# One instruction for a half block's normalization, ScalarE for the first output copies, and block 4's attention kept to the second group

## The chip, the cores and the metric

The program runs on one core of a Trainium2 chip. The metric is the time of one execution on the device, in microseconds; the median of several runs is quoted, and a profiled execution supplies the traces.

## What is computed

Attention over pooled keys and values, then a layer x -> (h cos h) with h = x w_in, then w_out, then a mixture of eight experts whose gate is balanced by eight rounds of row and column scaling. The change touches the first two stages:

```python
k_p = k.reshape(B, H, Sp, pool, D).mean(axis=3)
v_p = v.reshape(B, H, Sp, pool, D).mean(axis=3)
scores = scale * np.matmul(q, k_p.transpose(0, 1, 3, 2))
scores = scores - np.max(scores, axis=-1, keepdims=True)
attn = np.exp(scores)
attn = attn / (np.sum(attn, axis=-1, keepdims=True) + 1e-09)
out = np.matmul(attn, v_p)
...
h = x @ w_in
g = h * np.cos(h)
return g @ w_out
```

with 4 batches, 8 heads, 576 tokens, heads of 64, a pool of 8 (so 72 keys), and hidden widths of 2048 here and 1024 in each expert.

## The kernel before

The 2304 tokens are cut into six blocks of 384. Blocks 0 to 3 are the first group, 4 and 5 the second. Within a group the loop runs over four units of 512 hidden columns and, in each, over the group's blocks; one (unit, block) pair is a task, so the first group is tasks 0 to 15 and the second 16 to 23. A task is `hidden1` four times (f0 to f3: twelve matmuls each, in three passes of split fp32, then cosine work on ScalarE and VectorE, then the low part gl on GpSimd) and `output1` (four output chunks of twelve matmuls, added to `acc`). A task's `output1` is issued in the next task, behind its f0. f1 and f3 write the PSUM banks `ps_s`, which the attention's scores use too; f0 and f2 write `ps_h`.

Beside the tasks two queues are drained. `attn_queue` holds, for the blocks 1 to 5 and two half blocks g each (four heads), `attn_weights` (scores, maximum, exponential, sum, `normalize`) and `attn_values` (transposes and the product with the values); neighbours are swapped so that the weights of the next half block come ahead of the values of this one. `ATT` says how many entries a task takes at its start: 5, 4 and 4 in tasks 0 to 2, none in tasks 3 to 7, and one each from task 8 on, until the queue is empty. `conv_queue` turns the 64-bit weights of later units into fp32: two pieces per task in tasks 0 to 11, by ScalarE, five VectorE instructions, one GpSimd instruction (cw, L126) and a write to DRAM (`wa1f`, `wb1f`), from where `load_unit` fetches them for the first block of a unit.

The keys and values of a batch are pooled when a block first needs them: `load_k` issues four loads of 288 KB (kr), sums each on GpSimd in three instructions (L200 twice, L202) and copies the result by ScalarE into the block-diagonal tile kbd (L207) that the scores multiply; `load_v` does the like for values (vr, vs). Batch 3 is first needed by block 4. These loads and the raw weight tiles share one pool, `rawp`, of three buffers, and all are issued on SP's queue. `split` (L94 on ScalarE, L95 on GpSimd) makes the high and low part of a raw weight tile.

Each engine runs its instructions in the order that the tile scheduler wrote down when the program was built: it simulates the program and moves instructions, so an edit in one place moves others.

```python
engine = nc.vector if n > 4 else nc.gpsimd
for i in range(0, n, 4):
    r = slice(i, i + 4)
    engine.tensor_tensor(out=at[:, r], in0=at[:, r], in1=rs[:, r].to_broadcast([P, 4, SP]), op=ALU.mult)
```

Of the kernel before, what the change touches and what calls it, by code (L numbers as in the profile page):

```python
# [14 lines left out]
AF = mybir.ActivationFunctionType  # L15
ALU = mybir.AluOpType
# [4 lines left out]
SP = S // POOL  # L21
HP = H // 2
P = 128
# [7 lines left out]
NBLK = T // NB  # L31
# [27 lines left out]
def fused_kernel(ctx: ExitStack, tc: tile.TileContext, qT, kT, vT, v0, wa1, wb1, wa2, wb2, wg, out):  # L59
    nc = tc.nc  # L60
# [69 lines left out]
    def mm3(ps, pairs, part=None):  # L130

        n = len(pairs)
        for i in range(n) if part is None else part:
            (lh, ll), (rh, rl) = pairs[i]
            nc.tensor.matmul(out=ps, lhsT=lh, rhs=rh, start=(i == 0), stop=False)  # L135
            nc.tensor.matmul(out=ps, lhsT=lh, rhs=rl, start=False, stop=False)  # L136
            nc.tensor.matmul(out=ps, lhsT=ll, rhs=rh, start=False, stop=(i == n - 1))  # L137

    def mm3_first(ps, pairs):

        mm3(ps[0], pairs[0], range(FC - 1))
        mm3(ps[1], pairs[1], range(FC - 1))
        mm3(ps[0], pairs[0], range(FC - 1, FC))
        mm3(ps[1], pairs[1], range(FC - 1, FC))

    def x_tiles(j):
        hi = xp.tile([P, KC, NB], F32R, tag=f"xh{j}", name=f"xh{j}")
        lo = xp.tile([P, KC, NB], F32R, tag=f"xl{j}", name=f"xl{j}")
        return hi, lo
# [136 lines left out]
    def normalize(at, sm):  # L286

        nc.vector.tensor_scalar(
            out=sm, in0=sm, scalar1=EPS, scalar2=float(POOL), op0=ALU.add, op1=ALU.mult
        )  # L290
        n = sm.shape[1]
        rs = sp.tile([P, TPB * 4, 1], F32, tag="rs", name="rs")[:, :n]
        nc.vector.reciprocal(out=rs, in_=sm)
        engine = nc.vector if n > 4 else nc.gpsimd
        for i in range(0, n, 4):
            r = slice(i, i + 4)
            engine.tensor_tensor(out=at[:, r], in0=at[:, r], in1=rs[:, r].to_broadcast([P, 4, SP]), op=ALU.mult)  # L297

    ats = {}
    xts = {}  # L300
# [6 lines left out]
    def attn_first(qcs, g):  # L307

        at = at_tile(0, g)
        for i in range(TPB):  # L310
            ps = scores(i, g, qcs[i][:, 2 * g:2 * g + 2], (ps_s, "ps") if i % 2 == 0 else (ps_a, "pa"))
            mx = sp.tile([P, 4, 1], F32, tag="mx", name="mx")
            nc.vector.tensor_reduce(out=mx.rearrange("p h o -> p (h o)"), in_=ps, op=ALU.max, axis=AX.X,
                                    negate=True)
            nc.vector.tensor_scalar(out=mx, in0=mx, scalar1=SCALE, scalar2=None, op0=ALU.mult)
            sm = sp.tile([P, 4, 1], F32, tag="sm0", name="sm0")
            for h in range(4):
                nc.scalar.activation(out=at[:, i, h, :], in_=ps[:, h, :], func=AF.Exp, scale=SCALE,
                                     bias=mx[:, h, :], accum_out=sm[:, h, :])
            normalize(at[:, i], sm)  # L320

    def attn_weights(j, g):

        at = at_tile(j, g)
        for i in range(TPB):
            c = j * TPB + i
            for _, _, b in batch_runs(c * P, P):
                if b not in kpool:
                    load_k(b)
            qc = qp.tile([P, 2, P], F32, tag="qc", name="qc")  # L330
            nc.sync.dma_start(out=qc, in_=qT[:, c, 2 * g:2 * g + 2])
            ps = scores(c, g, qc)
            mx = sp.tile([P, 4, 1], F32, tag="mx", name="mx")
            nc.vector.tensor_reduce(out=mx.rearrange("p h o -> p (h o)"), in_=ps, op=ALU.max, axis=AX.X)
            nc.vector.tensor_tensor(out=at[:, i], in0=ps, in1=mx.to_broadcast([P, 4, SP]), op=ALU.subtract)
        nc.scalar.activation(out=at, in_=at, func=AF.Exp, scale=SCALE)
        sm = sp.tile([P, TPB * 4, 1], F32, tag="sm", name="sm")
        nc.vector.tensor_reduce(out=sm.rearrange("p h o -> p (h o)"), in_=at, op=ALU.add, axis=AX.X)
        normalize(at.rearrange("p c h s -> p (c h) s"), sm)
# [53 lines left out]
    def output1(j, u, gs, w_b, acc):  # L393

        last = u == U1 - 1
        if last:
            nhi, nlo = x_tiles(j)
        pss = {}

        def product(c):  # L400
            return [((w_b[f][0][:, c * P:(c + 1) * P], w_b[f][1][:, c * P:(c + 1) * P]), gs[f]) for f in range(FC)]

        for c in range(KC):
            if c == 0:
                for cc in range(2):
                    pss[cc] = ps_o.tile([P, 512], F32, tag="po", name="po")[:, :NB]
                mm3_first([pss[0], pss[1]], [product(0), product(1)])
            elif c > 1:
                pss[c] = ps_o.tile([P, 512], F32, tag="po", name="po")[:, :NB]
                mm3(pss[c], product(c))  # L410
            ps = pss[c]
            a = acc[:, c, :]
            if u == 0:
                nc.vector.tensor_copy(out=a, in_=ps)
            else:
                nc.vector.tensor_tensor(out=a, in0=ps, in1=a, op=ALU.add)
            if last:
                nc.scalar.activation(out=nhi[:, c, :], in_=a, func=AF.Copy)
                nc.vector.tensor_tensor(
                    out=nlo[:, c, :], in0=a, in1=nhi[:, c, :].bitcast(F32), op=ALU.subtract  # L420
                )
        if last:
            x1[j] = (nhi, nlo)
            if j > 1:
                nc.sync.dma_start(out=x1f[j], in_=acc)

    GRP = [[0, 1, 2, 3], [4, 5]]
# [9 lines left out]
    def convert_piece(u, i, raw=None):  # L437
        if raw is None:
            raw = load_piece(u, i)
        return convert(raw, (wa1f, wb1f)[i // FC], u, i % FC)  # L440

    attn_queue = [lambda f=f, j=j, g=g: f(j, g) for j in range(1, NBLK) for g in range(2)
                  for f in (attn_weights, attn_values)]

    for i in range(1, len(attn_queue) - 1, 2):
        attn_queue[i:i + 2] = attn_queue[i + 1], attn_queue[i]
    conv_queue = [lambda u=u, i=i: convert_piece(u, i) for u in range(1, U1) for i in range(2 * FC)]

    def run(queue, n):
        for _ in range(min(n, len(queue))):  # L450
            queue.pop(0)()
# [292 lines left out]
    pending = None  # L744
    task = 0

    ATT = [5, 4, 4, 0, 0, 0, 0, 0]
    accs = {}
    side = []
    for gi, grp in enumerate(GRP):  # L750
# [3 lines left out]
        for u in range(U1):  # L754
            for j in grp:
# [6 lines left out]
                if u == 0:  # L762
                    accs[j] = accp.tile([P, KC, NB], F32, tag="acc", name="acc")
                run(attn_queue, ATT[task] if task < len(ATT) else 1)
                gs = []
                for f in range(FC):
# [12 lines left out]
                    if f == 0 and j == GRP[1][1] and u == U1 - 1:  # L779
                        side.append(lambda: logits(GRP[1][0]))  # L780
                pending = lambda j=j, u=u, gs=gs, w=w_b, a=accs[j]: output1(j, u, gs, w, a)
                if gi == 1 and u == 0 and j == grp[0]:
                    x_op, x_load, x_todo = x_pieces(0)
# [11 lines left out]
    for _ in range(2):  # L795

        ps = ps_s.tile([P, 512], F32, tag="ps", name="pset")
# [94 lines left out]
```

## Time and profile before

| | us |
|---|---|
| median of 3 runs | 2053.98 (2053.37 to 2056.27) |
| the profiled execution | 2056.55 |
| its span, first to last instruction | 2054.7 |
| TensorE busy in the span | 2008.2 |
| VectorE / ScalarE / GpSimd busy | 1254.5 / 899.3 / 818.1 |

PE is TensorE, PEld its weight loads, DVE VectorE, ACT ScalarE, POOL GpSimd, SPq the DMA queue of SP. Names such as gl<-r,gh are the program's tiles, output first. A figure in brackets behind a row is how long the engine stood idle before it, and what released it. Matmuls are pipelined, so their starts tell their pace.

### The profile page before, as it was taken

Reading aid. Unit: us, or ns where it says so; the run is one execution under the profiler, and the core shown is the slowest. Engines: PE = TensorE matmul, PEld = TensorE weight load, DVE = VectorE, ACT = ScalarE, POOL = GpSimd, SP = SyncE. Lnnn points to the kernel's source line nnn. Section 1 sums busy time; section 2 is a strip of 40 time slices with the busy share of each in tenths; the row PEclk is TensorE's granted clock in tenths of the full one; section 3 lists DMA queues with packets and bytes.
Section 4 is the critical chain, followed back from the end, with each engine's and each line's share of the span. In section 5 each row is a group of like instructions: output and inputs, shape, how many; then the busy total and the mean of one; then the engine's idle time right before and its main releaser. Section 6 shows DMA issues by size and latency. Waiting matters only on the chain.

```text
span 2054.7 us, 27450 instructions
## 1 busy us (share of the span) xinstructions
PE 2008.2 (98%) x10339; PEld 1817.8 (88%) x10339; DVE 1254.5 (61%) x2003; ACT 899.3 (44%) x1781; POOL 818.1 (40%) x646
## 2 busy tenths in 40 slices
PE   6799999999999999999999999999999999999999
PEld 5689899999888889989888888888898888898887
DVE  8987785655685555555666555555565655555553
ACT  6675566656533334333444343343343343333431
POOL 7755653433333234243443342342353432433420
PEclk8899999999999999999999999999999999999999
DMA  7433331211311212212232122121132221221210
GB/s 257 140 126 124 110 121 47 83 52 62 123 63 62 68 56 82 62 62 74 70 123 72 52 83 72 52 82 62 62 107 92 69 72 54 80 72 52 83 42 31
DMA packets 53636, 167.46 MB, mean 81 GB/s; under 512 B 6112, under 2 KB 9952, under 8 KB 53504
## 3 DMA queue, kind: packets, MB, share of 16 engines
q1 hardware_dynamic: 53504, 165.72, 24.9%
q8 instruction: 81, 1.33, 0.3%
q14 instruction: 51, 0.42, 0.1%
HBM read 149.44 MB, written 16.25 MB: 81 GB/s over the span
## 4 chain that ended last, share of the span: by engine, by line
PE 88%; DVE 5%; DMA 1%; ACT 1%; issue 1%; POOL 1%; SPq 0%; DVEq 0%; ACTq 0%; POOLq 0%
PE po L135 15%; PE po L136 15%; PE po L137 15%; PE py L683 14%; PE pv L683 10%; PE px L683 10%; PE ph L136 2%; PE ph L135 2%; PE ph L137 2%; DVE m L121 1%; DVE at L297 1%; DVE cw L125 0%; DMA wb1f<-cw 0%; DVE m L119 0%; DVE r L387 0%
## 5 line engine op out<-in xcount | busy, mean ns | idle before, releaser
L95 POOL TENSOR_TENSOR wlo<-raw,whi 128x512 fp32r<-128x512 f32 x248 | 345.2, 1410 | 680.9 <-ACT gh L671 489.6
L135 PE MATMUL po<-whi,gh 128*128 128x512 f32 x1152 | 455.1, 395 | 0.6 <-DVE acc L733 0.6
L136 PE MATMUL po<-wlo,gh 128*128 128x512 f32 x1152 | 454.4, 394 | 0.0
L137 PE MATMUL po<-whi,gl 128*128 128x512 f32 x1152 | 454.0, 394 | 0.0
L94 ACT ACTIVATE whi<-raw 128x512 fp32r<-128x512 f32 x488 | 290.3, 625 | 220.6 <-PE py L683 184.8
L739 DVE SCALAR_TENSOR_TENSOR acc<-po,pr,acc 128x512 f32<-128x512 f32 x252 | 188.7, 749 | 292.4 <-PE po L137 288.2
L683 PE MATMUL py<-xc,whi 128*128 128x384 f32 x1152 | 293.7, 335 | 0.0
L95 DVE TENSOR_TENSOR wlo<-raw,whi 128x512 fp32r<-128x512 f32 x240 | 216.7, 903 | 125.6 <-ACT whi L94 60.5
L137 PEld LDWEIGHTS po<-whi,gl 128*128 128x128 f32 x1152 | 216.2, 188 | 50.1
L135 PEld LDWEIGHTS po<-whi,gh 128*128 128x128 f32 x1152 | 216.1, 188 | 42.3 <-DVE acc L733 0.8
L136 PEld LDWEIGHTS po<-wlo,gh 128*128 128x128 f32 x1152 | 215.7, 187 | 37.9
L683 PEld LDWEIGHTS py<-xc,whi 128*128 128x128 f32 x1152 | 210.1, 188 | 12.3
L683 PE MATMUL py<-xc,wlo 128*128 128x384 f32 x576 | 192.7, 335 | 0.0
L587 POOL TENSOR_TENSOR s<-raw 128x512 f32<-128x512 f32 x48 | 63.2, 1317 | 312.1 <-DMA raw<-wa 288.9
L683 PE MATMUL pv<-xc,whi 128*128 128x384 f32 x640 | 169.4, 338 | 2.0 <-DVE gl L672 2.0
L671 ACT ACTIVATE gh<-c 128x384 fp32r<-128x384 f32 x96 | 50.2, 523 | 224.2 <-DVE c L711 224.2
L135 PE MATMUL ph<-xh,whi 128*128 128x384 f32 x384 | 130.3, 343 | 5.1 <-DVE r L387 5.0
L683 PE MATMUL px<-xc,whi 128*128 128x384 f32 x512 | 134.8, 335 | 0.0
L136 PE MATMUL ph<-xl,whi 128*128 128x384 f32 x384 | 130.6, 341 | 0.7 <-DVE xl L368 0.7
L136 PE MATMUL po<-gl,whi 128*128 128x384 f32 x384 | 129.2, 337 | 0.6 <-POOL gl L390 0.6
L137 PE MATMUL ph<-xh,wlo 128*128 128x384 f32 x384 | 129.2, 337 | 0.0
L137 PE MATMUL po<-gh,wlo 128*128 128x384 f32 x384 | 128.3, 337 | 0.0
(161 smaller groups left out, 3635.9 us busy)
## 6 DMA issues: line engine op xcount, KB each, us to landing
raw<-wa SPq DMA_DIRECT2D x112, 512.0 KB, 4.5
raw<-wb SPq DMA_DIRECT2D x112, 512.0 KB, 3.6
raw<-wa1f SPq DMA_DIRECT2D x14, 512.0 KB, 3.7
raw<-wb1f SPq DMA_DIRECT2D x14, 512.0 KB, 3.7
out<-acc SPq DMA_DIRECT2D x18, 256.0 KB, 4.3
wa1f<-cw SPq DMA_DIRECT2D x16, 256.0 KB, 2.9
wb1f<-cw SPq DMA_DIRECT2D x16, 256.0 KB, 2.8
qc<-qt SPq DMA_DIRECT2D x30, 128.0 KB, 4.2
```

Of the source, the lines that this page charges most:

```text
L94: nc.scalar.activation(out=hi, in_=src, func=AF.Copy)
L95: lo_engine.tensor_tensor(out=lo, in0=src, in1=hi.bitcast(F32), op=ALU.subtract)
L121: v.scalar_tensor_tensor(out=m, in0=high, scalar=-2**30, in1=m, op0=ALU.bitwise_and, op1=ALU.bitwise_or)
L135: nc.tensor.matmul(out=ps, lhsT=lh, rhs=rh, start=(i == 0), stop=False)
L136: nc.tensor.matmul(out=ps, lhsT=lh, rhs=rl, start=False, stop=False)
L137: nc.tensor.matmul(out=ps, lhsT=ll, rhs=rh, start=False, stop=(i == n - 1))
L297: engine.tensor_tensor(out=at[:, r], in0=at[:, r], in1=rs[:, r].to_broadcast([P, 4, SP]), op=ALU.mult)
L587: nc.gpsimd.tensor_tensor(out=out, in0=x, in1=y, op=op)
L671: nc.scalar.activation(out=gh, in_=c, func=AF.Relu)
L683: marks["pe"] = nc.tensor.matmul(out=ps, lhsT=l[:, k], rhs=r[:, c, :], start=(start and c + n == 0), stop=(last and n == 2), skip_group_ch ...
L739: nc.vector.scalar_tensor_tensor(out=a, in0=po, scalar=pe, in1=a, op0=ALU.mult, op1=ALU.add)
```

## The change

Three edits. `normalize` multiplies all 12 groups of 72 weights of a half block in one instruction of 128x864 instead of three of 128x288 (block 0, with four groups at a time on GpSimd, is as before). In `output1` the outputs of the first unit are copied from PSUM to `acc` by ScalarE instead of VectorE. And the attention queue is built from two parts, the blocks 1 to 3 and the blocks 4 and 5, each with its own swaps: the first part's twelve entries are taken in tasks 0 to 2 (5, 4, 3), and the second part's eight in tasks 8 to 15. Before, the weights of block 4's first half were taken in task 2, with the keys of batch 3.

```diff
--- before.py
+++ after.py
@@ -292,9 +292,7 @@
         rs = sp.tile([P, TPB * 4, 1], F32, tag="rs", name="rs")[:, :n]
         nc.vector.reciprocal(out=rs, in_=sm)
         engine = nc.vector if n > 4 else nc.gpsimd
-        for i in range(0, n, 4):
-            r = slice(i, i + 4)
-            engine.tensor_tensor(out=at[:, r], in0=at[:, r], in1=rs[:, r].to_broadcast([P, 4, SP]), op=ALU.mult)
+        engine.tensor_tensor(out=at, in0=at, in1=rs.to_broadcast([P, n, SP]), op=ALU.mult)
 
     ats = {}
     xts = {}
@@ -411,7 +409,7 @@
             ps = pss[c]
             a = acc[:, c, :]
             if u == 0:
-                nc.vector.tensor_copy(out=a, in_=ps)
+                nc.scalar.activation(out=a, in_=ps, func=AF.Copy)
             else:
                 nc.vector.tensor_tensor(out=a, in0=ps, in1=a, op=ALU.add)
             if last:
@@ -439,11 +437,13 @@
             raw = load_piece(u, i)
         return convert(raw, (wa1f, wb1f)[i // FC], u, i % FC)
 
-    attn_queue = [lambda f=f, j=j, g=g: f(j, g) for j in range(1, NBLK) for g in range(2)
-                  for f in (attn_weights, attn_values)]
-
-    for i in range(1, len(attn_queue) - 1, 2):
-        attn_queue[i:i + 2] = attn_queue[i + 1], attn_queue[i]
+    attn_queue = []
+    for blocks in (GRP[0][1:], GRP[1]):
+        part = [lambda f=f, j=j, g=g: f(j, g) for j in blocks for g in range(2) for f in (attn_weights, attn_values)]
+
+        for i in range(1, len(part) - 1, 2):
+            part[i:i + 2] = part[i + 1], part[i]
+        attn_queue += part
     conv_queue = [lambda u=u, i=i: convert_piece(u, i) for u in range(1, U1) for i in range(2 * FC)]
 
     def run(queue, n):
@@ -744,7 +744,7 @@
     pending = None
     task = 0
 
-    ATT = [5, 4, 4, 0, 0, 0, 0, 0]
+    ATT = [5, 4, 3, 0, 0, 0, 0, 0]
     accs = {}
     side = []
     for gi, grp in enumerate(GRP):
```

In the printed orders below, line numbers of the changed kernel between 295 and 438 are two lower for the same statement. On VectorE, in task 0, the first normalization of block 1 (at is its weights, rs the reciprocal sums); before:

```order
L125 SCALAR_TENSOR_TENSOR cw_397<-raw64_394,cw_397 128x512
L297 TENSOR_TENSOR at_459<-at_459,rs_513 128x288 x3
L121 SCALAR_TENSOR_TENSOR m_412<-raw64_410,m_412 128x512
L334 TENSOR_REDUCE mx_616<-psc_613 128x4
L335 TENSOR_TENSOR at_518<-psc_539,mx_542 128x288
```

and in the changed kernel:

```order
L125 SCALAR_TENSOR_TENSOR cw_397<-raw64_394,cw_397 128x512
L295 TENSOR_TENSOR at_459<-at_459,rs_513 128x864
L121 SCALAR_TENSOR_TENSOR m_412<-raw64_410,m_412 128x512
L332 TENSOR_REDUCE mx_612<-psc_609 128x4
L333 TENSOR_TENSOR at_516<-psc_537,mx_540 128x288
```

Three instructions became one and nothing else moved there.

On GpSimd, in task 8, from the last converted piece of unit 2 (cw) and the low part of f0 (gl) on; before:

```order
L126 TENSOR_TENSOR cw_2356<-m_2355,cw_2356 128x512
L390 TENSOR_TENSOR gl_2461<-r_2454,gh_2460 128x384
L200 TENSOR_TENSOR vr_2616<-vr_2616 72x512
L95 TENSOR_TENSOR wlo_2392<-raw_2385,whi_2391 128x512
L200 TENSOR_TENSOR vr_2616<-vr_2616 72x256
L95 TENSOR_TENSOR wlo_2398<-raw_2395,whi_2397 128x512
L95 TENSOR_TENSOR wlo_2402<-raw_2395,whi_2401 128x512
L202 TENSOR_TENSOR vs_2615<-vr_2616 72x128
L200 TENSOR_TENSOR vr_2621<-vr_2621 72x512
L200 TENSOR_TENSOR vr_2621<-vr_2621 72x256
L390 TENSOR_TENSOR gl_2540<-r_2533,gh_2539 128x384
```

and in the changed kernel:

```order
L126 TENSOR_TENSOR cw_2285<-m_2284,cw_2285 128x512
L388 TENSOR_TENSOR gl_2411<-r_2404,gh_2410 128x384
L200 TENSOR_TENSOR kr_2344<-kr_2344 128x288
L200 TENSOR_TENSOR kr_2344<-kr_2344 128x144
L202 TENSOR_TENSOR ks_2343<-kr_2344 128x72
L95 TENSOR_TENSOR wlo_2321<-raw_2314,whi_2320 128x512
L95 TENSOR_TENSOR wlo_2327<-raw_2324,whi_2326 128x512
L200 TENSOR_TENSOR kr_2349<-kr_2349 128x288
L95 TENSOR_TENSOR wlo_2331<-raw_2324,whi_2330 128x512
L200 TENSOR_TENSOR kr_2354<-kr_2354 128x288
L200 TENSOR_TENSOR kr_2349<-kr_2349 128x144
L200 TENSOR_TENSOR kr_2354<-kr_2354 128x144
```

The key sums of batch 3 now stand there, the value sums behind them, and the low part of f1 comes 29 instructions behind that of f0 instead of nine.

On TensorE, in the same place, behind the first output products of task 8 (po with gl of f0); before:

```order
L135 MATMUL po_2693<-gh_2460,whi_2387 128x384
L136 MATMUL po_2693<-gl_2461,whi_2387 128x384
L137 MATMUL po_2693<-gh_2460,wlo_2388 128x384
L360 MATMUL px_2655<-pt_2636,vs_2615 64x192 x2
L135 MATMUL ph_2748<-xh1_554,whi_2371 128x384
```

and in the changed kernel:

```order
L135 MATMUL po_2621<-gh_2410,whi_2316 128x384
L136 MATMUL po_2621<-gl_2411,whi_2316 128x384
L137 MATMUL po_2621<-gh_2410,wlo_2317 128x384
L277 MATMUL psc_2368<-kbd1_128,qc_2366 64x144
L277 MATMUL psc_2368<-kbd0_126,qc_2366 64x144
L277 MATMUL psc_2368<-kbd1_128,qc_2366 64x144
L277 MATMUL psc_2378<-kbd1_128,qc_2376 128x144 x2
L135 MATMUL ph_2470<-xh0_278,whi_2300 128x384
```

Block 4's first scores, on the keys of batch 3 (kbd1), stand where a product with batch 3's values stood; the hidden products f1 (ph_2470) and f3 of task 8 come behind them.

## Rows read from the trace of the kernel before

**Rows 1.** The page, busy time of each engine over the whole span.

```profile
PE 2008.2 (98%) x10339; PEld 1817.8 (88%) x10339; DVE 1254.5 (61%) x2003; ACT 899.3 (44%) x1781; POOL 818.1 (40%) x646
```

**Rows 2.** Windows: stretch, us, busy us by engine, granted clock, DMA share, GB/s.

```profile
47.00:100.00 53.00, 41.59 (x231) 34.39 (x230) 52.36 (x83) 31.54 (x54) 41.77 (x45) 0.86 0.52 156
100.00:130.00 30.00, 28.17 (x170) 24.13 (x169) 27.11 (x58) 21.83 (x39) 16.38 (x18) 1.00 0.50 156
...
220.00:262.00 42.00, 36.88 (x217) 33.24 (x216) 35.68 (x52) 22.38 (x44) 27.56 (x26) 1.00 0.39 118
...
620.00:2055.00 1435.00, 1430.97 (x7108) 1280.13 (x7107) 794.29 (x1157) 534.80 (x1038) 506.27 (x362) 1.00 0.22 70
```

**Rows 3.** Timeline of VectorE: start, us, engine, line, operation, names, shapes, count.

```profile
47.71 5.34 DVE L297 TENSOR_TENSOR at<-at,rs 128x288 f32<-128x288 f32 x3
...
60.47 3.04 DVE L297 TENSOR_TENSOR at<-at,rs 128x288 f32<-128x288 f32 x3
...
76.69 3.37 DVE L297 TENSOR_TENSOR at<-at,rs 128x288 f32<-128x288 f32 x3
...
118.22 1.20 DVE L297 TENSOR_TENSOR at<-at,rs 128x288 f32<-128x288 f32 x3
```

**Rows 4.** Windows of L297 alone: busy us of VectorE and of GpSimd, clock, DMA.

```profile
47.00:112.00 65.00, 16.56 (x15) 0.00 (x0) 0.89 0.53 158
```

**Rows 5.** Groups by line and form, 0 to 420 us: count | busy, mean ns | idle before.

```profile
L95 POOL TENSOR_TENSOR wlo<-raw,whi 128x512 fp32r<-128x512 f32 x37 | 51.3, 1395 | 49.3 <-PE po L136 14.9 <-PE ph L137 12.9 <-ACT whi L94 10.5
...
L367 ACT ACTIVATE xh<-px 128x384 fp32r<-128x384 f32 x24 | 11.4, 480 | 5.7 <-PE px L360 5.7
...
L414 DVE COPY acc<-po 128x384 f32<-128x384 f32 x20 | 10.7, 547 | 4.0 <-PE po L137 3.9
L338 DVE TENSOR_REDUCE sm<-at 128x12 f32<-128x864 f32 x10 | 10.5, 1046 | 4.2 <-ACT at L336 4.0
```

**Rows 6.** The same view: the key sums and the copies of the keys.

```profile
L200 POOL TENSOR_TENSOR kr<-kr 128x288 f32<-128x288 f32 x12 | 11.1, 929 | 0.4 <-DMA kr<-kt 0.4
...
L200 POOL TENSOR_TENSOR kr<-kr 128x144 f32<-128x144 f32 x12 | 7.6, 638 | 0.1
...
L202 POOL TENSOR_TENSOR ks<-kr 128x72 f32<-128x72 f32 x12 | 6.2, 516 | 0.1
...
L207 ACT ACTIVATE kbd<-ks 64x288 f32<-64x288 f32 x6 | 2.6, 436 | 0.0
```

**Rows 7.** The tile of a key load (kr): time from its issue to its landing.

```profile
DMA to landing us min/median/max: 2.9/3.7/4.5
```

**Rows 8.** Timeline of GpSimd in task 8, with idle time before and its releaser.

```profile
224.68 1.28 POOL L126 TENSOR_TENSOR cw<-m,cw 128x512 f32<-128x512 f32 x1 [1.14 <-issue]
...
236.19 1.29 POOL L200 TENSOR_TENSOR vr<-vr 72x512 f32<-72x512 f32 x1 [9.26 <-DMA vr<-vt]
```

**Rows 9.** Timeline of SP's DMA queue in the same place.

```profile
226.96 0.43 SPq L127 DMA_DIRECT2D wb1f<-cw  x1
230.69 0.33 SPq L102 DMA_DIRECT2D raw<-wb1f  x1
231.06 12.63 SPq L265 DMA_DIRECT2D vr<-vt  x4
```

**Rows 10.** TensorE's timeline: task 7's last hidden product, and two later rows.

```profile
217.74 0.34 PE L137 MATMUL ph<-xh,wlo 128*128 128x384 f32 x1
...
219.46 0.33 PE L135 MATMUL ph<-xh,whi 128*128 128x384 f32 x1
219.63 0.33 PE L136 MATMUL ph<-xl,whi 128*128 128x384 f32 x1
```

**Rows 11.** Timeline of TensorE after its longest wait ahead of 100 us.

```profile
43.69 1.30 PE L277 MATMUL psc<-kbd,qc 128*128 128x144 f32 x4 [5.67 <-DVE at L335]
...
47.51 0.49 PE L136 MATMUL ph<-xl,whi 128*128 128x384 f32 x1
47.83 0.35 PE L137 MATMUL ph<-xh,wlo 128*128 128x384 f32 x1
```

## The prediction, made before the changed kernel ran

> **What bounds the kernel now.** I read the table of busy time first: TensorE is busy for 98% of the span [rows 1], so a change can win only where TensorE is idle, and every new idle stretch is paid in full. The windows say where: after 620 us nothing is open (1430.97 of 1435 us), and between 47 and 100 us TensorE is busy for 41.59 of 53 us, at a granted clock of 0.86, while VectorE is busy for 52.36 [rows 2]. There VectorE bounds. From 100 to 130 us only 1.8 us are open, and between 220 and 262 us it is 5.1 us [rows 2]. The printed orders of the two programs agree again after some 2,960 of 10,165 matmuls, where the expert stage begins, so everything happens in the first 600 us.
>
> **The change, part by part.**
>
> *One normalization instead of three.* Ten times, three multiplications of 128x288 become one of 128x864. Undisturbed, three take 1.20 us (the row at 118.22); the first three groups take 5.34, 3.04 and 3.37 us [rows 3], and the 15 instructions between 47 and 112 us take 16.56 us [rows 4]. What is over 5 x 1.20 = 6.0 us, 10.6 us or 0.70 us for each instruction, falls in a stretch in which GpSimd is busy for 41.77 of 53 us [rows 2]. No row has one multiplication of 864 columns; the nearest is the sum over 864 columns, 1.05 us [rows 5]. If the one instruction waits as long as one of the three did, five cost 5 x 1.75 = 8.7 us and 7.8 us go away; if it waits as long as three together, 5 x 1.05 + 10.6 = 15.8 us, and 0.8 us goes; if it never waits, 11.3 us. The first row speaks for the middle: the waits came to each of the three anew. The Trainium skill (SBUF — State Buffer, "Who interferes with whom") says that a VectorE instruction with two SBUF inputs and a GpSimd instruction lock each other out for the whole instruction. By that rule the one waits for at most one GpSimd instruction, 1.40 us for the longest group [rows 5], and at least 16.6 - 5 x 2.45 = 4.3 us would go; the trace has waits that look longer than one instruction (5.34 us for three), so I don't lean on it.
>
> Only what lies ahead of 100 us counts in full, since TensorE is nearly full behind it. The first three groups sum to 11.75 us and would be 3 x 1.75 = 5.2 us: 6.5 us less, under 11.4 us of open TensorE time. I take -7 us for this part, with 0 and -11.4 us as ends.
>
> *First outputs copied by ScalarE.* 24 copies of 128x384 leave VectorE at 0.547 us each; ScalarE does the same shape out of PSUM in 0.480 us [rows 5]. They begin at 95 us, where TensorE has little left to win, and ScalarE is busy for 21.83 of 30 us [rows 2], so it can take four per task. I take 0, between -1 and +8 us (the last is a rival below).
>
> *Block 4's first weights, moved from task 2 to task 8.* With it goes the loading of the keys of batch 3: four loads of 288 KB, twelve sums on GpSimd (4 x (0.929 + 0.638 + 0.516) = 8.3 us) and two copies on ScalarE (0.436 us each) [rows 6]. Block 4 is the first that needs batch 3. Taking this out of 90 to 130 us relieves VectorE and GpSimd where TensorE has 1.8 us open: -1 us, between 0 and -2.
>
> What it adds stands in task 8, and here I expect the loss. Task 8 is where the weights of unit 2 arrive, through the same three raw buffers, and the key loads stand behind them on SP's queue. The trace of before has the same chain with value loads in the place of the key loads: GpSimd finishes the last converted piece at 225.96 us, its write is issued at 226.96, the weight load behind that write at 230.69, the first value load at 231.06, and GpSimd, idle for 9.26 us, starts on it at 236.19 [rows 8, 9]. In the changed order the first key load stands there, so I put its first sum at 236.2 us as well. GpSimd then has, in its printed order, the 8.3 us of key sums with three weight splits among them (3 x 1.40 us [rows 5]), 12.5 us. Two loads must be waited for besides: the second key load reuses the buffer that the first of these splits frees, the third the buffer that the last one frees, and a key load takes 2.9 to 4.5 us to land, median 3.7 [rows 7]. Of the first, one split hides 1.4 us; of the second nothing is hidden. That is 2.3 + 3.7 = 6.0 us. The keys are then summed at 236.2 + 12.5 + 6.0 = 254.7 us and copied at 255.6.
>
> When does TensorE need them? In the changed order the first scores on these keys stand 117 rows behind the last hidden product of task 7. That product ended at 218.1 us, and a row takes 0.173 us [rows 10]: TensorE is there at 218.1 + 20.2 = 238.3 us. It has no way around them, as its queue is in order, and the hidden products behind them (f1 and f3 of task 8) take the banks of these very scores. Stall: 255.6 - 238.3 = 17.3 us. The ends: 19 us with landings of 4.5 us; 10.5 us if landings take 2.9 us, the sums run faster while VectorE idles, and the chain begins 3 us earlier because VectorE is less busy.
>
> Next in line: behind the key copies ScalarE's queue has the exponentials of these weights, then the cosine work of four hidden products that TensorE finished before the stall or just behind it, some 17 instructions of about 0.5 us [rows 5], 8.5 us, until the attention values can be multiplied; TensorE has 24 products and twelve transposes under that, 5.5 us. I take 3 us, between 0 and 8. And the clock: after 5.67 us of idleness TensorE's matmuls came 0.32 us apart instead of 0.17, until 47.8 us, as at the lower of its two clocks (1.2 instead of 2.4 GHz), some 4 us long [rows 11], a loss of 2 us; I take 2, between 0 and 4. Against this, the 5.1 us that TensorE now loses between 220 and 262 us [rows 2] go, since they stem from the same place: the value sums and splits that crowd GpSimd from 236 us on [rows 8].
>
> **The sum.** 17.3 + 3 + 2 - 5.1 = +17.2 us in task 8, -7 - 1 = -8 us before, together **+9 us**. On the profiled execution, 2056.55 us (span 2054.7), that is 2065.6; the median of the runs is 2053.98, 2.6 us lower, so I predict **2063 us**. Its own range, -4 to +20 us, takes the ends of the stall against those of the first stretch: 2050 to 2074.
>
> **Rivals.**
>
> 1. *The key chain is covered, only the gain stays.* If the key loads land before TensorE gets to the scores, or TensorE arrives late there for other reasons, -8 us are left: 2046 us. For it: the first stretch's gain rests on measured groups, and GpSimd was 9.26 us idle just ahead of the chain. Against it: that idleness is spent waiting for the very load behind which the keys stand, and TensorE would need over 17 us of other work. It decides if the keys are copied before 240 us on this trace's clock. Chance 0.22.
>
> 2. *ScalarE becomes the one that holds output banks.* Two banks take the outputs, and a copy now stands in ScalarE's queue, perhaps behind a table load and an exponential. With 16 copies in the first group, half of them 1 us late, 8 us come on top of the forecast: 2071 us. For it: ScalarE at 21.83 of 30 us [rows 2]; against it: the order puts these copies right behind short instructions. It decides where ScalarE has over half a microsecond in front of a copy when the product ends. Chance 0.10.
>
> 3. *The two sums cancel*: the stall at its low end (10.5 us, nothing behind it, +5.4 us) and a first stretch of -5 us: no change, 2054 us. Chance 0.10.
>
> **How the numbers follow.** The forecast has 0.58. A measurement of this kernel can tell 0.2%, 4.1 us, from no change. Of the forecast's chance 0.46 lie above that, 0.11 within, 0.01 below. Rival 1 gives 0.19 faster and 0.03 same, rival 2 0.10 slower, rival 3 0.10 same. Together: slower 0.56, same 0.24, faster 0.20. The range runs from 2045 us, which takes in half of rival 1 and more, to 2074 us, the high end of the forecast's own; about 0.15 is left outside.
>
> **What would show it.** Right: a wait of TensorE's scores (L277) in task 8 on GpSimd's key sums or ScalarE's key copy, over 10 us in one piece, near 230 us on the new clock; GpSimd in a row of key sums and value sums there, idle on key loads twice; and an idle share between 47 and 100 us that falls from 11.4 us to about 4, with single normalizations of about 1.75 us. Wrong: no wait over 5 us in task 8, or key sums that end before TensorE's scores; or normalizations that still take 3 to 5 us each. The copies at L412 should show no wait of output products (L135 po) over 1 us.

## The result, and the profile after

| | before | changed |
|---|---|---|
| median, us (5 runs each) | 2053.98 (2052.97 to 2056.27) | 2069.04 (2068.51 to 2071.26) |
| ratio, 95% interval | | 1.0071 [1.0061, 1.0082] |
| the profiled execution, us | 2056.55 | 2071.26 |
| its span, us | 2054.7 | 2069.3 |

The change costs 0.71%, 15 us; 9 us were forecast. The windows of the changed kernel answer to [rows 2]. The columns are the same: stretch, length, busy time of TensorE, its weight loads, VectorE, ScalarE and GpSimd with counts, granted clock, DMA share, GB/s.

```profile
47.00:100.00 53.00, 44.42 (x225) 36.77 (x225) 49.30 (x73) 32.27 (x56) 44.26 (x43) 0.78 0.47 144
100.00:130.00 30.00, 28.21 (x170) 24.97 (x169) 22.71 (x44) 24.63 (x47) 9.33 (x9) 1.00 0.41 128
...
220.00:262.00 42.00, 27.40 (x146) 24.65 (x146) 20.52 (x36) 15.47 (x29) 26.96 (x33) 0.83 0.38 113
...
620.00:2055.00 1435.00, 1434.48 (x7126) 1283.77 (x7127) 801.40 (x1171) 542.64 (x1052) 513.78 (x367) 1.00 0.22 70
```

Behind 620 us nothing is open, as before. Between 220 and 262 us TensorE is now busy for 27.40 us and not 36.88. Between 47 and 100 us it is idle for 8.6 us and not 11.4, but its clock is lower, 0.78 and not 0.86: it is busy longer and has done fewer matmuls, 225 and not 231.

Idle time alone doesn't tell where the 14.6 us between the two spans went, since the clock differs too. So I gave every matmul its spacing at full clock (the median over both traces for its tile and shape), summed this over TensorE's order as the work done, and compared when each trace had done as much. The table is this lag behind the profiled execution of before, in us, at points on the time of before. It is good to about 1 us, since the orders differ locally.

| kernel | 98 | 130 | 178 | 226 | 274 | 520 | end |
|---|---|---|---|---|---|---|---|
| changed | 1.0 | 0.6 | 0.7 | 4.7 | 18.8 | 17.5 | 14.5 |
| normalization alone | 5.6 | 5.5 | 5.6 | 5.6 | 6.5 | 6.7 | 3.2 |
| copies alone | -0.4 | 1.8 | 1.7 | 2.7 | 2.9 | 2.7 | -1.2 |
| queue alone | 1.3 | -0.3 | 2.8 | 3.2 | 21.8 | 22.2 | 19.1 |
| normalization and copies | -1.8 | -0.7 | -1.3 | -1.3 | -0.9 | -0.3 | -2.8 |
| changed, keys early | 1.2 | 2.5 | 2.7 | 4.9 | 5.2 | 6.7 | 2.3 |
| changed, weights in task 5 | 1.7 | 1.2 | 4.1 | 11.3 | 11.1 | 12.3 | 7.9 |
| changed, weights in task 3 | 1.3 | 0.3 | -0.3 | -0.3 | 0.2 | 0.9 | -1.7 |
| no multiplications | -3.7 | 1.5 | 2.8 | 3.4 | 2.8 | 5.3 | 1.9 |
| fewer sums on GpSimd | -4.8 | -2.8 | -3.8 | -2.5 | -6.0 | -4.3 | -8.4 |

Three things stand in the first row. The gain that was forecast ahead of 130 us isn't there. Task 8, between 226 and 274 us, costs 14.1 us. And between 178 and 226 us there are 4 us that I had not forecast. The last column is some 3 us lower than the one before it in every row; the profiled execution of before is itself 2.6 us over its median, so I read that step, near 550 us, as time lost in that execution and not as a gain of the ten kernels in the table.

**Task 8.** GpSimd's timeline in the changed kernel, which answers to [rows 8]:

```profile
225.18 1.29 POOL L126 TENSOR_TENSOR cw<-m,cw 128x512 f32<-128x512 f32 x1 [1.14 <-issue]
...
234.38 1.39 POOL L200 TENSOR_TENSOR kr<-kr 128x288 f32<-128x288 f32 x2 [5.45 <-DMA kr<-kt]
...
236.14 2.49 POOL L95 TENSOR_TENSOR wlo<-raw,whi 128x512 fp32r<-128x512 f32 x2
239.20 0.79 POOL L200 TENSOR_TENSOR kr<-kr 128x288 f32<-128x288 f32 x1 [0.56 <-DMA kr<-kt]
239.95 1.26 POOL L95 TENSOR_TENSOR wlo<-raw,whi 128x512 fp32r<-128x512 f32 x1
...
244.19 1.36 POOL L200 TENSOR_TENSOR kr<-kr 128x288 f32<-128x288 f32 x2 [0.76 <-DMA kr<-kt]
245.63 0.34 POOL L202 TENSOR_TENSOR ks<-kr 128x72 f32<-128x72 f32 x1
```

It is the row of key sums with three weight splits among them, idle on key loads twice more, as forecast. On SP's queue, answering to [rows 9], the key loads stand right behind the weight load, as the value loads did:

```profile
226.50 0.33 SPq L127 DMA_DIRECT2D wb1f<-cw  x1
229.77 0.33 SPq L102 DMA_DIRECT2D raw<-wb1f  x1
230.14 11.42 SPq L257 DMA_DIRECT2D kr<-kt  x4
```

TensorE's timeline shows the product ahead of the scores, one of the first output products of task 8, and the wait; the last row is one of the hidden products behind it, 0.32 us after the one before it, where 0.17 is the spacing at full clock:

```profile
236.46 0.33 PE L137 MATMUL po<-gh,wlo 128*128 128x384 f32 x1
246.94 2.48 PE L277 MATMUL psc<-kbd,qc 128*64 128x144 f32 x10 [10.15 <-ACT kbd L207]
...
250.08 0.52 PE L137 MATMUL ph<-xh,wlo 128*128 128x384 f32 x1
```

The windows behind the wait show the clock, at half its rate (1.2 of 2.4 GHz) until 251.5 us and a second time after 258.3 us:

```profile
247.00:251.50 4.50, 4.50 (x17) 3.91 (x18) 1.93 (x5) 2.11 (x2) 4.50 (x5) 0.50 0.40 121
251.50:258.30 6.80, 5.01 (x35) 4.36 (x33) 6.70 (x11) 4.94 (x11) 5.51 (x8) 1.00 0.17 45
258.30:268.50 10.20, 7.67 (x32) 6.09 (x29) 8.20 (x16) 6.80 (x14) 6.77 (x7) 0.50 0.48 158
```

**The normalizations.** VectorE's timeline, which answers to [rows 3]:

```profile
48.52 3.52 DVE L295 TENSOR_TENSOR at<-at,rs 128x864 f32<-128x864 f32 x1
61.04 1.30 DVE L295 TENSOR_TENSOR at<-at,rs 128x864 f32<-128x864 f32 x1
77.69 1.19 DVE L295 TENSOR_TENSOR at<-at,rs 128x864 f32<-128x864 f32 x1
...
118.28 1.06 DVE L295 TENSOR_TENSOR at<-at,rs 128x864 f32<-128x864 f32 x1
```

The first five take 8.3 us and not 16.6 us [rows 4]: the 8.7 us that I took were right. Yet the sixth starts at 118.28 us, where it started at 118.22 before [rows 3]. What took the gain is in the experiments.

### The profile page after: what moved, and what is told of

It is laid out like the page before. It is cut to its first block, busy times and chain, and to the rows that moved or that the text cites. A ratio compares the mean times of both kernels' runs of the same rounds, so it can differ in the third digit from the quotient of the medians.

```text
span 2069.3 us, 27439 instructions
## 1 busy us (share of the span) xinstructions
PE 2014.2 (97%) x10339; PEld 1823.1 (88%) x10339; DVE 1235.2 (60%) x1959; ACT 910.9 (44%) x1805; POOL 819.9 (40%) x646
## 4 chain that ended last, share of the span: by engine, by line
PE 89%; DVE 4%; ACT 2%; DMA 2%; issue 1%; POOL 0%; SPq 0%; POOLq 0%; ACTq 0%; DVEq 0%
PE po L135 16%; PE po L136 16%; PE po L137 15%; PE py L683 14%; PE px L683 10%; PE pv L683 9%; PE ph L135 2%; PE ph L136 2%; PE ph L137 2%; PE px L358 1%; DMA kr<-kt 0%; DVE m L121 0%; PE psc L277 0%; PE pl L508 0%; DVE m L117 0%
## 5 line engine op out<-in xcount | busy, mean ns | idle before, releaser
L135 PE MATMUL po<-gh,whi 128*128 128x384 f32 x384 | 129.1, 345 | 3.2 <-DVE acc L414 1.8
```

## The experiments

Ratios are to runs of the kernel before on the same chip, whose medians there were 2054.8 to 2055.3 us.

**1. The normalization alone.**

```diff
-        for i in range(0, n, 4):
-            r = slice(i, i + 4)
-            engine.tensor_tensor(out=at[:, r], in0=at[:, r], in1=rs[:, r].to_broadcast([P, 4, SP]), op=ALU.mult)
+        engine.tensor_tensor(out=at, in0=at, in1=rs.to_broadcast([P, n, SP]), op=ALU.mult)
```

> The kernel before with the one normalization instead of three, nothing else. Theory A (the gain of the first stretch exists, and the copies on ScalarE or the new queue took it away again in the changed kernel): the five normalizations ahead of 112 us fall from 16.6 us to about 8.3 us, TensorE is 6 to 7 us earlier by 130 us, and the time is about 2047 us. Theory B (the shorter instruction frees VectorE, but TensorE there then waits for something else, and its slow clock lasts as long): the normalizations are as short, TensorE is within 2 us of the kernel before at 130 us, and the time is 2052 to 2056 us.

Measured: 2058.69 us, 1.0018 [1.0009, 1.0027]. Neither theory had it slower. The five normalizations take 10.5 us, and TensorE's lag grows from -1.1 us at 82 us to 5.6 us at 98 us. Its timeline has one long wait there:

```profile
94.38 0.69 PE L135 MATMUL ph<-xh,whi 128*128 128x384 f32 x1 [6.33 <-DVE r L385]
```

The product r (L385) that it waits for stands in VectorE's queue, at 93.78 us, behind these rows of VectorE's timeline; the conversion's step L119 takes 0.43 us at the median of its 32 in the kernel before:

```profile
88.66 2.03 DVE L119 TENSOR_SCALAR m<-m 128x512 int32<-128x512 int32 x1
90.61 0.44 DVE L332 TENSOR_REDUCE mx<-psc 128x4 f32<-128x288 f32 x1
90.98 1.74 DVE L295 TENSOR_TENSOR at<-at,rs 128x864 f32<-128x864 f32 x1
92.65 0.44 DVE L332 TENSOR_REDUCE mx<-psc 128x4 f32<-128x288 f32 x1
93.01 0.84 DVE L121 SCALAR_TENSOR_TENSOR m<-raw,m 128x512 int32<-128x512 int32 x1
```

**2. The copies alone.**

```diff
-                nc.vector.tensor_copy(out=a, in_=ps)
+                nc.scalar.activation(out=a, in_=ps, func=AF.Copy)
```

> The kernel before with the first outputs copied by ScalarE, nothing else. Theory (the copies are neutral, and norm and copies together gave no change because the one normalization alone had lost 3 us by its order): 2052 to 2056 us. Rival (the copies are what brings the pair back, since VectorE is 0.55 us shorter for each of 24): 2048 to 2051 us.

Measured: 2056.78 us, 1.0006 [0.9997, 1.0015]. By themselves the copies do nothing that can be measured.

**3. The queue alone** (the new construction of `attn_queue`, and ATT = [5, 4, 3, ...]).

> The kernel before with the new queue alone (three multiplications, copies on VectorE). Theory of the key chain: TensorE's scores wait about 10 us for the copy of batch 3's keys in task 8, with slow clock behind it; the time is 2065 to 2070 us, as in the changed kernel. Rival (the chain is as late only because the copies on ScalarE and the new order around them let TensorE run ahead): a wait below 5 us and 2055 to 2060 us.

Measured: 2075.27 us, 1.0101 [1.0087, 1.0115], more than the whole change and above the ranges of both theories. The wait on the key copy is 13.23 us, with another of 4.8 us behind it, in TensorE's timeline:

```profile
248.52 2.48 PE L277 MATMUL psc<-kbd,qc 128*64 128x144 f32 x10 [13.23 <-ACT kbd L207]
...
262.53 1.33 PE L277 MATMUL psc<-kbd,qc 128*128 128x144 f32 x4 [4.79 <-DVE r L387]
```

So the stall needs neither of the other two edits.

**4. Normalization and copies, with the old queue.**

```diff
-    ATT = [5, 4, 3, 0, 0, 0, 0, 0]
+    ATT = [5, 4, 4, 0, 0, 0, 0, 0]
...
+    attn_queue = [lambda f=f, j=j, g=g: f(j, g) for j in range(1, NBLK) for g in range(2)
+                  for f in (attn_weights, attn_values)]
...
```

> The changed kernel with the queue and the numbers of the kernel before: batch 3's keys are loaded in task 2 again. Theory of the key chain: what the queue costs is gone, and the other two parts give 0 to -7 us: 2047 to 2055 us, no wait over 5 us on the key copies. Rival (the copies on ScalarE hold TensorE, as at 184 us of the changed kernel, where it waited 1.8 us for an output bank and then ran 3.4 us at the slow clock): 2057 to 2060 us.

Measured: 2053.42 us, 0.9995 [0.9986, 1.0003]: no change. The queue is what makes the changed kernel slow: 1.0071 less 0.9995 is 0.76%, 15.6 us. Together the other two gain nothing, though the normalization alone loses 0.18%. The product r starts only 1.3 us earlier (at 92.45 us and not at 93.78); what differs is TensorE's order. In experiment 1 the hidden product that waits for r stands right behind the two output products of 87.42 us. Here the scheduler put 24 output products ahead of the hidden products, and TensorE's timeline has in the place of the 6.33 us a wait for an output bank that ScalarE's copy (acc, L412) holds:

```profile
89.33 0.45 PE L135 MATMUL po<-gh,whi 128*128 128x384 f32 x1 [2.43 <-ACT acc L412]
```

**5. The changed kernel with batch 3's keys loaded in task 2.**

```diff
         attn_queue += part
+        if blocks[0] == 1:
+            attn_queue.append(lambda: load_k(3))
...
-    ATT = [5, 4, 3, 0, 0, 0, 0, 0]
+    ATT = [5, 4, 4, 0, 0, 0, 0, 0]
```

> The changed kernel, with batch 3's keys loaded, summed and copied in task 2 as the thirteenth step, while block 4's first weights stay in task 8. Theory of the key chain: the 10 us wait on the key copy goes, and with it the slow clock behind it, 13 to 14 us: 2055 us. Rival (the weights themselves crowd task 8: their scores, exponential and sums stand in the queues of VectorE and ScalarE ahead of the hidden products' cosine work): another wait of 5 to 10 us takes its place, and the time is 2062 to 2069 us.

Measured: 2059.77 us, 1.0028 [1.0016, 1.0041]; of 0.71% some 0.43%, 9 us, is gone, and the time lies between those of the theory and the rival. No wait on a key copy is left in task 8, whose cost falls from 14.1 us of lag to 0.3 (4.9 at 226 us, 5.2 at 274). What takes its place in TensorE's timeline is shorter:

```profile
246.09 0.69 PE L135 MATMUL po<-gh,whi 128*128 128x384 f32 x1 [3.56 <-DVE acc L414]
```

That addition (L414) stands on VectorE behind a conversion step that takes 0.68 us at its shortest. Here it lasts 6.38 us, while GpSimd, from 239.08 to 245.02 us, runs five instructions without a break:

```profile
239.19 6.38 DVE L121 SCALAR_TENSOR_TENSOR m<-raw,m 128x512 int32<-128x512 int32 x1
```

The chain is the cause of the stall, then, and the rival has the smaller part. What remains over the kernel before had mostly been lost by 226 us (4.9 us of lag there).

**6 and 7. Block 4's first weights in task 5, and in task 3.**

```diff
-    ATT = [5, 4, 3, 0, 0, 0, 0, 0]
+    ATT = [5, 4, 3, 0, 0, 1, 0, 0]
```

and, in the other kernel,

```diff
-    ATT = [5, 4, 3, 0, 0, 0, 0, 0]
+    ATT = [5, 4, 3, 1, 0, 0, 0, 0]
```

> The changed kernel with block 4's first weights, and with them batch 3's keys, in task 5 in the place of task 8; tasks 3 to 7 have no other attention step. Theory of the key chain: there the loads have no value loads and no other scores beside them, but the same three raw buffers and unit 1's weights are on the queue; if TensorE has over 15 us of hidden and output products ahead of the scores the wait is gone and the time is 2053 to 2057 us. Rival (any place with unit weights on the queue ahead makes TensorE wait at the scores, as the queue is in order): a wait of 3 to 10 us there and 2059 to 2066 us.

> The same with block 4's first weights in task 3, right behind the first group's attention and ahead of unit 1's weights. Theory of the key chain: no unit weights stand ahead of the keys on the queue, so no wait over 3 us on the key copy: 2050 to 2056 us. Rival (task 3 is still crowded on VectorE, and what the queue gave up in task 2 comes back one task later): 2057 to 2062 us.

Measured: in task 5 2062.56 us, 1.0036 [1.0024, 1.0049]; in task 3 2054.49 us, 0.9996 [0.9987, 1.0005]. In task 5 the time is the rival's, but not the wait: TensorE never waits at the scores. Several short waits, 5.4 us together between 160 and 230 us and none over 1.93, and some 3 us at half clock make up the 7 us of lag that come between 178 and 226 us. In task 3 the queue's whole cost is gone: the scheduler put the key sums of batch 3 between 99 and 114 us, and TensorE never waits for them.

**8. No multiplications at all.** The kernel before without them.

```diff
-        for i in range(0, n, 4):
+        for i in range(0, n if n == 4 else 0, 4):
```

> The kernel before without the multiplications of the normalization (the three of each half block of blocks 1 to 5 are left out, so the attention weights stay unnormalized there). They are 16.6 us of VectorE between 47 and 112 us, 10.6 of it waiting. Theory that the waiting is carried over: it belongs to GpSimd's work, which is unchanged, so that the conversion's instructions on VectorE (mantissa and exponent steps, 128x512) wait some 4 us longer, VectorE is 8 to 12 us less busy, and TensorE gains at most 3 us by 130 us: 2051 to 2056 us. Rival (the waiting goes with the instructions that waited): the conversion's instructions keep their durations, and 7 to 11 us are won: 2043 to 2047 us.

Measured: 2056.37 us, 1.0010 [1.0001, 1.0019]: taking all 16.6 us away gains nothing either. The groups of VectorE's conversion steps between 47 and 112 us show where the waiting went (count | busy us, mean ns). The kernel before:

```profile
L121 DVE SCALAR_TENSOR_TENSOR m<-raw,m 128x512 int32<-128x512 int32 x7 | 7.1, 1013 | 0.0
L125 DVE SCALAR_TENSOR_TENSOR cw<-raw,cw 128x512 f32<-128x512 uint32 x7 | 5.9, 839 | 0.0
L119 DVE TENSOR_SCALAR m<-m 128x512 int32<-128x512 int32 x6 | 5.1, 856 | 0.0
L124 DVE TENSOR_SCALAR cw<-m 128x512 int32<-128x512 int32 x6 | 4.5, 753 | 0.0
L117 DVE TENSOR_SCALAR m<-m 128x512 f32<-128x512 f32 x6 | 3.9, 653 | 0.0
```

The changed kernel, with one multiplication in the place of three:

```profile
L121 DVE SCALAR_TENSOR_TENSOR m<-raw,m 128x512 int32<-128x512 int32 x7 | 8.0, 1136 | 0.0
L125 DVE SCALAR_TENSOR_TENSOR cw<-raw,cw 128x512 f32<-128x512 uint32 x7 | 7.6, 1079 | 0.0
L119 DVE TENSOR_SCALAR m<-m 128x512 int32<-128x512 int32 x7 | 5.2, 744 | 0.0
L117 DVE TENSOR_SCALAR m<-m 128x512 f32<-128x512 f32 x6 | 5.2, 865 | 0.0
L124 DVE TENSOR_SCALAR cw<-m 128x512 int32<-128x512 int32 x6 | 5.1, 842 | 0.0
```

Without any:

```profile
L124 DVE TENSOR_SCALAR cw<-m 128x512 int32<-128x512 int32 x7 | 9.0, 1285 | 0.0
L121 DVE SCALAR_TENSOR_TENSOR m<-raw,m 128x512 int32<-128x512 int32 x7 | 8.8, 1263 | 0.0
L119 DVE TENSOR_SCALAR m<-m 128x512 int32<-128x512 int32 x7 | 8.0, 1143 | 0.0
L125 DVE SCALAR_TENSOR_TENSOR cw<-raw,cw 128x512 f32<-128x512 uint32 x6 | 5.7, 959 | 0.0
L117 DVE TENSOR_SCALAR m<-m 128x512 f32<-128x512 f32 x6 | 2.9, 486 | 0.0
```

The steps' mean goes from 26.5 / 32 = 0.83 us to 31.1 / 33 = 0.94 and 34.4 / 33 = 1.04 us. Against the same 33 steps at 0.83 us that is 3.7 us more in the changed kernel, where the multiplications lost 8.3, and 7.0 us more here, where 16.6 went. Nearly half of what is taken away comes back, in the next instructions of the same queue. TensorE is 5.6 us ahead at 82 us and has lost it again by 106 us, in waits of 2.5 and 1.1 us and 6.8 us at half clock. The wait of 2.5 us ends at 93.95 us, 0.1 us after a subtraction of VectorE (L335) that stood behind conversion steps of 2.47, 1.11 and 0.94 us; but the profile names no releaser for it, and which instruction bounds that stretch was not settled.

**9. Fewer sums on GpSimd.** The kernel before, with GpSimd doing one of three additions.

```diff
-        n = POOL // 2
+        n = POOL // 2 if engine is nc.vector else 1
```

> The kernel before with only the last of the three sums of each key and value load on GpSimd (the first two are left out, so only two of the eight rows are summed). Three quarters of GpSimd's summing time goes, in the first stretch some 10 us, and no instruction of VectorE. Theory (the waiting on VectorE belongs to GpSimd's work): VectorE's instructions ahead of 112 us lose 5 us or more of their waiting, the multiplications of the normalization and the conversion's steps alike, and 3 to 7 us are won: 2047 to 2051 us. Rival (the stretch is bound by a chain through TensorE and ScalarE as well, as the run without multiplications suggests): VectorE is less busy as said, and the time is within 2 us of the kernel before: 2053 to 2057 us.

Measured: 2048.19 us, 0.9966 [0.9953, 0.9979], 7 us faster, with every instruction of VectorE in place. Its window shows GpSimd at 23.61 us in the place of 41.77 [rows 2]:

```profile
47.00:100.00 53.00, 44.98 (x255) 38.51 (x253) 50.28 (x94) 37.06 (x61) 23.61 (x24) 0.88 0.49 153
```

In as long a stretch VectorE did 94 instructions and not 83, and TensorE 255 matmuls and not 231. The first five groups of multiplications take 10.6 us and not 16.6, and the conversion's steps 0.74 us in the mean and not 0.83 (L125 alone grows). The rival falls. Only a part is the gain that I had looked for in the normalization: the lag is -2.8 us at 130 us. Another 3.5 us come in task 8, between 226 and 274 us, where TensorE no longer waits the 1.6 us that the kernel before waits for GpSimd's value sums (vs, L202). The run doesn't separate what VectorE waits less from what GpSimd's own sums take less. It is no version to keep, since only two of eight rows are summed.

TensorE's order is another one than in the kernel before in experiments 1, 8 and 9 alike, from 63, 44 and 28 us on. The difference between experiments 1 and 4, nearly 5 us, came with such a change of order, so that none of these three times is free of it.

**10. The keys of task 8 summed by VectorE** (TensorE's order is the changed kernel's row by row).

```diff
-            pool_sum(ks[:, hp], kr, nc.gpsimd)
+            pool_sum(ks[:, hp], kr, nc.vector if b == 3 else nc.gpsimd)
```

> The changed kernel with the sums of batch 3's keys (those of task 8) on VectorE, where the first of them takes 0.46 us in place of 0.93 us; TensorE's order is the same row by row. Theory A (the chain's length is the sums and the splits between them on GpSimd): the key copies come 3 to 6 us earlier, TensorE's wait falls from 10.2 to 4 to 7 us, 2062 to 2066 us. Theory B (its length is the loads, each waiting for a raw buffer and some 3.7 us to land): the wait stays at 8 to 10 us, and the additions of outputs that now stand behind key sums on VectorE's queue hold output banks: 2067 to 2072 us.

Measured: 2067.07 us, 1.0059 [1.0045, 1.0073]. The waits in TensorE's timeline:

```profile
236.61 0.41 PE L135 MATMUL po<-gh,whi 128*128 128x384 f32 x1 [3.07 <-DVE acc L414]
240.56 0.69 PE L135 MATMUL po<-gh,whi 128*128 128x384 f32 x1 [3.19 <-DVE acc L414]
245.18 2.48 PE L277 MATMUL psc<-kbd,qc 128*64 128x144 f32 x10 [3.29 <-ACT kbd L207]
```

They are 9.55 us together and not 10.15, and the time is theory B's; the wait on the key copy alone is shorter than either theory had it, since TensorE comes to it later by the other two. The key copies come at 244.2 us and not 246.0, but this run stood 1.8 us earlier already at 226 us (lag 2.9 and not 4.7). With shorter sums, the waits for loads behind the first grow from 1.3 to 4.3 us. So the loads set the length of the chain, and the additions of outputs behind the key sums now hold TensorE too.

**11. Weights in task 3, and the copies on VectorE again.**

```diff
-                nc.scalar.activation(out=a, in_=ps, func=AF.Copy)
+                nc.vector.tensor_copy(out=a, in_=ps)
```

> The changed kernel with block 4's first weights in task 3 and the copies of first outputs on VectorE again. In the run with the copies on ScalarE, TensorE waited 3.0 us at 90 us for an output bank that ScalarE's copy held behind a table load of 1.28 us. Theory (that wait is the copies' price and goes with them): 2050 to 2053 us. Rival (without the copies on ScalarE the first stretch loses as much on VectorE, as in the run with the normalization alone): 2056 to 2060 us.

Measured: 2058.33 us, 1.0016 [1.0007, 1.0024]. The rival was right: as in experiment 1, the lag jumps between 82 and 98 us, from -1.2 to 4.8 us. With the one normalization, the copies on ScalarE are worth some 4 us; without it, nothing. It is again TensorE's order: here, too, the hidden products that wait for r stand ahead of the output products, and with the copies on ScalarE (experiments 4 and 7) behind them.

No version was found that is measurably faster than the kernel before and computes the same; experiments 4 and 7 equal it.

## Why the prediction was right, and where its size was off

The direction was right, and so was its reason; the time, 2069 us, lies in the range. By the steps of the prediction:

- *Block 4's first weights.* Right. Experiments 3, 4, 5 and 7 put the loss there: 15.6 us with the queue against none without it (good to some 3 us by the two intervals; alone, the queue cost 21 us), where I had 17.2 - 1 = 16.2 us. That the two agree so closely is in part luck, since the terms inside were off both ways. The first key sum starts at 234.4 us (236.2 forecast), and TensorE is at the scores at 236.8 us (238.3). The chain to the copies' end takes 12.5 us and not 19.4: the sums take 6.5 us for 8.3, and the two waits for loads 1.3 us for 6.0. The stall is 10.15 us, the low end that I had named (10.5) and not the 17.3 that I took. Against that, the clock cost more than the 2 us that I took: at half clock TensorE was busy for 4.50 us and, a second time, for 7.67 us, and half of that is 6 us. The waits behind the stall are 1.5, 0.3 and 2.5 us, 4.3 us for 3. Less the 5.1 us of old waits: 10.2 + 6 + 4.3 - 5.1 = 15.4 us, where the lag says 14.1. The reason that I gave for the old waits holds only in part: 1.6 us were for GpSimd's value sums, 3.5 us for VectorE's product r (L387).
- *One normalization instead of three.* **This is the step that failed.** The price of the instruction was right (8.3 us for 8.7, and 16.6 before). "6.5 us less, under 11.4 us of open TensorE time. I take -7 us" was not: experiments 1, 4 and 8 show that TensorE gains nothing, even where all 16.6 us go. I took the waiting as the multiplications' own. Experiments 8 and 9 speak for its belonging to the work of GpSimd: nearly half of what is taken away comes back in the conversion's steps that follow in the queue, and with 18 us less of GpSimd's work it shrinks. What holds TensorE for the rest stays open, and so does the part of the changed order. The Trainium skill (SBUF — State Buffer, "Who interferes with whom") says that copies and tensor_scalar operations of VectorE can contend with GpSimd, as instructions with two SBUF inputs do; the trace agrees, since in experiment 8 the tensor_scalar steps L119 and L124 grow from 0.86 and 0.75 us to 1.14 and 1.29. And I counted idle time of TensorE without its clock: it fell by 2.8 us, to 8.6 and not to the 4 that I had named as a sign, and the clock of the same 53 us fell from 0.86 to 0.78, most of all between 82 and 98 us (0.68 for 0.89).
- *First outputs copied by ScalarE.* Taken as 0; alone 0.06%, within the interval of no change. That they would matter through the order that the scheduler gives TensorE (experiments 1, 4 and 11) I had not seen. Rival 2's mechanism occurs (2.4 and 3.0 us of waiting for L412 in experiments 4 and 7), at a third of its price, and hardly in the changed kernel (0.8 us in all).
- *Between 178 and 226 us* the changed kernel loses 4 us that no step had: TensorE waits 1.78 us for an addition of outputs (L414) behind conversion steps on VectorE and then runs at half clock for 3.4 us. The wait is there in experiment 5 too (1.9 us, at full clock); in experiments 3 and 4 TensorE waits for nothing between 170 and 226 us. So neither the queue alone nor the other two edits alone bring it, and why the order of all three together does stays open.
- *The sum.* The -7 of the normalization came out as about -1 (experiment 4, within the interval of no change), the 16.2 as 15.6: +9 forecast, +15 measured.

## What to carry to other kernels

Before counting the waiting of an instruction as a gain, ask whose work it waits for: here nearly half of what was taken off VectorE came back in the next instructions of its queue, and TensorE won nothing from the rest. Where a scheduler orders the program, compare the orders of the other engines too before an edit gets the credit: the 4 us of the copies were an order. And before moving a step to a later place, follow its loads through the queue and the buffers they share, to the first product that needs them: here the same step cost 15 us in task 8, 8 us in task 5 and nothing in task 3.

## What the hardware showed that I had not expected

One VectorE instruction can wait through several GpSimd instructions in a row. In experiment 8 a conversion step that takes 0.43 us at the median in the kernel before took 4.00 us, by VectorE's timeline:

```profile
83.95 4.00 DVE L119 TENSOR_SCALAR m<-m 128x512 int32<-128x512 int32 x1
```

By GpSimd's timeline, it ran three instructions over the same time, one right behind another, none over 1.3 us:

```profile
83.89 2.54 POOL L200 TENSOR_TENSOR vr<-vr 72x512 f32<-72x512 f32 x2 [1.70 <-DMA vr<-vt]
86.37 1.29 POOL L95 TENSOR_TENSOR wlo<-cw,whi 128x512 fp32r<-128x512 f32 x1
```

So the one instruction doesn't wait "for at most one GpSimd instruction", the bound that I had drawn from the rule of the Trainium skill (SBUF — State Buffer, "Who interferes with whom") and set aside. Instructions with two SBUF inputs do the same: L121 in experiment 5 (6.38 us), and the first normalization of the changed kernel, 3.52 us where 1.05 is the shortest, during which three GpSimd instructions end, at 48.91, 50.15 and 51.11 us. The other surprise is the clock: it fell a second time, at 258.3 us, after TensorE had been back at work at full clock since 251.5 us with 1.8 us of waits, and the second stretch at half clock, 10.2 us, cost more than the first.
